# Scale and bias of the activations applied to each tile by ScalarE, in place of scaled PSUM reads and a bias row

## The chip, the cores and the metric

The kernel runs on one core of a Trainium2 chip. The metric is the device time of one execution in microseconds. Before the change it is 912.62 us, the median of three runs (911.99, 912.62, 912.62). The profile shown below is of one further execution, which took 912.49 us; its recorded span is 910.7 us, and the granted TensorE clock was 1.0 over the whole of it.

## The reference

An attention without softmax over 8 batches, 8 heads, 576 tokens and 64 channels feeds a two-layer network over 4608 tokens:

```python
kv  = k.T @ v                                  # per head, over its 576 tokens
out = q @ kv                                   # per head
x   = out / sqrt(mean(out^2) + 1e-6) * g_norm  # then (B, H, S, D) -> (4608, 512)
h   = x @ w_in                                 # (4608, 512) @ (512, 2048)
r   = maximum(h, 0)
g   = s * (r * r) + b                          # s and b: one number each
y   = g @ w_out                                # (4608, 2048) @ (2048, 512)
```

Nearly all the arithmetic is in the two products `x @ w_in` (the first stage) and `g @ w_out` (the second). Since s and b are single numbers, `g @ w_out` equals s times `(r * r) @ w_out` plus b times the column sums of `w_out`: s and b may be applied to the tiles of r*r, or after the second product.

## The kernel before, in words

**Tiling.** The 4608 tokens are 36 chunks of 128, worked on in nine units (0 to 8) of four chunks. In each unit the first stage makes the activations of 512 tokens in four steps of 512 hidden columns; a step gives four tiles, called a11, a12, a21 and a22, of 128 partitions by 512 elements each: two blocks of hidden columns by 256 tokens. (`s` in names such as `s1` counts steps or sums and has nothing to do with the factor s, which stands in `s_col`.) The second stage then multiplies the tiles by w_out.

**Fewer products by the Strassen-Winograd scheme.** A product of matrices cut in 2 x 2 blocks is done as seven products in place of eight, at the price of sums of blocks ahead of and after them. The products are numbered; in a family of seven, products 1, 6, 5 and 3 run into one PSUM bank of tag x, one after the other, each added to what is there, and the bank is read out after each of them; product 2 goes to a bank of tag z; 7 and then 4 go to a bank of tag y. So a bank x that was read by ScalarE or VectorE late makes the next product of its family wait. Unit 0 has a plain first stage (`mm1_plain`, 16 slots, one for each tile, while the weights arrive and are converted from 64 to 32 bits beside it) and one level of the scheme in the second stage. Unit 1 has one level in both (`mm1`, `mm2`). Units 2 to 8 have two levels in the second stage and in part of the first (`mm1_deep`, `at_two_levels`; the weight sums are stored in DRAM once and streamed through a ring of buffers for every unit). There the functions of a family are called `sums_i` (sums of tiles), `do_i` (product and read-out), `go_i` (product alone) and `out_i` (read-out alone), where i is the product of the outer level; `do_1(6)` is inner product 6 of outer product 1.

**Order.** Everything lies under a manual schedule: the program's text fixes the order of instructions of each engine, and an engine takes its own instructions one after the other. Only waits for data and for buffers move things in time. In a deep unit the order is `run` in `mm1_deep` and then `rest` in `mm2`; in units 0 and 1 it is the lists that `mm2` returns and the loop at the end of the kernel. Attention of the next unit is put in between by `at(n)`, by numbered places.

**Activation tiles.** h comes out of PSUM as a sum of what the scheme keeps in tiles. r*r is made in place. On VectorE it is one operation, `relu_sq` (L667, (max(t, 0) times t)). On ScalarE it is a Relu and a Square (L815 and L816 for tiles in SBUF, L861 and L862 for a21 out of PSUM, both in deep units). L849 and L836 are copies of an x bank by ScalarE in a deep unit, L715 is such a copy in unit 1. After r*r come sums of tiles: s1 = a21 + a22 (L250), then differences for the other products (L253). In the deep units a second layer of sums of these (`sums_1`, `sums_25` and so on) is done by VectorE just ahead of the inner products.

**Where s and b enter.** The tiles hold r*r, without s and b. Every read-out of a PSUM bank in the second stage multiplies by s on its way: `scaled` (L1099) is one VectorE operation that computes PSUM times s plus another tile, 128 or 256 elements wide. b enters by a row: `column_sums` adds up the rows of w_out within each partition as the weights of unit 0 arrive (16 operations of VectorE), and `bias_row` (L353 to L361) makes b times the whole column sums of it with one matrix product (into b_ps), a copy to `b_row` (L360) and a difference `b_21` of its halves. `b_row` then is the "other" tile of the first read-outs of every unit, and in deep units `start_5` copies b_21 by ScalarE (L1351) into two quarters of the output tiles, as the value that product 5 starts from. L91 is the one line from which nearly all matmuls are issued.

**Other lines that are spoken of.** L519 scales x by g_norm, four ScalarE operations for 256 tokens. L587 is the Square of the attention's norm. L478 and L568 are parts of the attention. L225 and L230 (ScalarE), L235 and L245 (VectorE) convert the weights in unit 0. The q loads are issued by GpSimd (L1640), as are the stores of the output in units 0 to 7 (L1215).

Of the kernel before, what the change touches and what calls it, by code (L numbers as in the profile page):

```python
# [16 lines left out]
def kernel(  # L17
# [291 lines left out]
    def column_sums(s, lower):  # L309

        w = w_dn if lower else w_up
        for b in range(2):
            f = 2 * s + b
            if f == 0 and not lower:
                nc.vector.tensor_copy(out=b_row, in_=w[:, f])
            else:
                add(b_row, b_row, w[:, f])

# [31 lines left out]
    b_sq = const.tile([P, P], FP32, name="b_sq")  # L350
    nc.vector.memset(b_sq, 1.0)
    b_row = const.tile([P, DM], FP32, name="b_row")
    b_21 = const.tile([P, HN], FP32, name="b_21")  # L353

    def bias_row():

        nc.vector.tensor_scalar(out=b_sq, in0=b_sq, scalar1=b_col, scalar2=None, op0=ALU.mult)
        ps = ps_t.tile([P, DM], FP32, name="b_ps", tag="t")
        matmul(ps, b_sq, b_row, True, True)
        nc.scalar.copy(b_row, ps)  # L360
        sub(b_21, b_row[:, HN:], b_row[:, :HN])  # L361

# [303 lines left out]
    def relu_sq(t):  # L666
        nc.vector.scalar_tensor_tensor(t, t, 0.0, t, ALU.max, ALU.mult)  # L667

# [6 lines left out]
    def g_s1(s):  # L675
        add(ga["s1", s], ga["a21", s], ga["a22", s])

    def mm1_plain(s):


        def block(lower, half, name, tag):
            ps = bank_of("c", tag)
            w = (wb if lower else wa)[s]
            for c in range(KC):
                for b in range(2):
                    matmul(
                        ps[:, b, :], w[:, c, b], xT[0][:, c, half * TB : half * TB + TB],
                        b == 0 and c == 0, c == KC - 1,
                    )
            def out_of():  # L690
                t = g_tile(name, s)
                nc.scalar.activation(t, ps, AF.Relu)
                nc.vector.tensor_mul(t, t, t)

            return out_of

        def c22():
            block(1, 1, "a22", "y")()
            g_tile("s1", s)
            g_s1(s)  # L700

        return [
            lambda: block(0, 0, "a11", "x"),
            lambda: block(1, 0, "a12", "y")(),
            lambda: block(0, 1, "a21", "x")(),
            c22,
        ]

    def mm1(u, s):

        st = {}

        def keep(name, src, tag):
            st[name] = rp.tile([P, 2, TB], FP32, name=name, tag=tag)
            nc.scalar.copy(st[name], src)  # L715

        def x1():
            st["x"] = bank_of("x", "x")
            mm1_product(1, u, s, st["x"], True)
            keep("r1", st["x"], "ra")  # L720

        def z2():
            ps = bank_of("z", "z", 1)
            mm1_product(2, u, s, ps, True)
            t = g_tile("a11", s)
            add(t, ps, st["r1"])
            relu_sq(t)

        def x6():
            mm1_product(6, u, s, st["x"], False)  # L730
            keep("r2", st["x"], "rb")

        def y7():
            st["y"] = bank_of("y", "y")
            mm1_product(7, u, s, st["y"], True)

        def x5():
            mm1_product(5, u, s, st["x"], False)
            keep("r4", st["x"], "ra")
            t = g_tile("a22", s)  # L740
            add(t, st["y"], st["r4"])
            if u > 1 and s == NS - 1:
                nc.scalar.activation(t, t, AF.Relu)
                nc.scalar.square(t, t)
            else:
                relu_sq(t)

        def x3():
            mm1_product(3, u, s, st["x"], False)
            nc.scalar.activation(g_tile("a21", s), st["x"], AF.Relu)  # L750

        def x3_square():
            if u > 1 and s == NS - 1:
                nc.scalar.square(ga["a21", s], ga["a21", s])
            else:
                nc.vector.tensor_mul(ga["a21", s], ga["a21", s], ga["a21", s])

        def x3_s1():
            g_tile("s1", s)
            g_s1(s)  # L760

        def x3_s3():
            sub(ga["a21", s], ga["a11", s], ga["a21", s])

        def y4():
            mm1_product(4, u, s, st["y"], False)
            add(g_tile("a12", s), st["y"], st["r2"])

        def y4_square():
            t = ga["a12", s]  # L770
            if u > 1 and s == NS - 1:
                nc.scalar.activation(t, t, AF.Relu)
                nc.scalar.square(t, t)
            else:
                relu_sq(t)

        return dict(
            x1=x1, z2=z2, x6=x6, y7=y7, x5=x5, x3=x3, x3_square=x3_square, x3_s1=x3_s1,
            x3_s3=x3_s3, y4=y4, y4_square=y4_square,
        )  # L780

# [27 lines left out]
    def mm1_deep(u):  # L809
# [3 lines left out]

        def relu_sq_on_act(t):
            nc.scalar.activation(t, t, AF.Relu)  # L815
            nc.scalar.square(t, t)  # L816
# [34 lines left out]
        def a22(s):  # L851
            t = g_tile("a22", s)
            add(t, st["y", s], ga["a21", s])
            if s == NS - 1:
                relu_sq_on_act(t)
            else:
                relu_sq(t)

        def x3(s):
            mm1_product(3, u, s, st["x", s], False)  # L860
            nc.scalar.activation(ga["a21", s], st["x", s], AF.Relu)  # L861
            nc.scalar.square(ga["a21", s], ga["a21", s])  # L862

        def y4(s):
# [5 lines left out]
            else:  # L870
                relu_sq(t)
# [58 lines left out]

        def done(name, *steps):
# [3 lines left out]
        def run(at, early, sums):  # L935
# [14 lines left out]
            x6(1)  # L950
            small(2, 0, 3, 4)
# [6 lines left out]
            x5(1)  # L958
            a22(1)
# [4 lines left out]
            x1(3)  # L964
            y4(1)
# [5 lines left out]
            x6(2)  # L971
            at(14)
            small(3, 0, 3, 4)
            x6(3)
            done("a21", 0, 1)
            at(15)
            small(2, 1, 1, 2)
            x5(2)
            s1(0)
# [3 lines left out]
            a22(2)  # L983
            y7(3)
# [6 lines left out]
            at(18)  # L991
            y4(2)
            done("a11", 2)
            s1(2)
            x5(3)
            done("a11", 3)
            a22(3)
# [5 lines left out]
            x3_square=lambda: None, y4_square=lambda: None,  # L1003
# [73 lines left out]
    def mm2(u, step=None, side={}):  # L1077
# [20 lines left out]
        def scaled(o, ps, other):  # L1098
            nc.vector.scalar_tensor_tensor(o, ps, s_col, other, ALU.mult, ALU.add)  # L1099

        b1, b2 = b_row[:, :HN], b_row[:, HN:]
# [18 lines left out]
        def at_two_levels(group, other, to):  # L1120
# [48 lines left out]
            def keep(name, j, q):  # L1169
# [4 lines left out]
                scaled(r[name], t["x"], other(j, cols[q]))  # L1174

            def out_of(m, k=slice(0, n)):
                if m == 1:
                    keep("r1", 0, 0)
                elif m == 2:
                    scaled(to(0, cols[0]), t["z"], r["r1"])  # L1180
                elif m == 6:
                    keep("r2", 1, 0)
                elif m == 5:
                    keep("r4", 1, 1)
                    scaled(to(1, cols[1]), t["y"], r["r4"])
                elif m == 3:
                    scaled(to(0, cols[1]), t["x"], other(0, cols[1]))
                elif m == 4:
                    scaled(to(1, cols[0])[:, k], t["y"][:, k], r["r2"][:, k])
# [8 lines left out]
        def part(name, j, ps, other):  # L1198
# [3 lines left out]
            scaled(st[name, j], ps, other)  # L1202
# [19 lines left out]
        def x1(j):  # L1222
            st["x", j] = half(("x", j), "x")
            product(1, j, st["x", j], True)
            if u > 0:
                part("r1", j, st["x", j], b1)

        def early_5(j):
# [3 lines left out]
            nc.scalar.activation(rows("o1", j)[:, HN:], ps, AF.Copy, scale=s_col)  # L1232

        def with_bias():
            bias_row()
            for j in range(2):
                part("r1", j, st["x", j], b1)
            for j in range(2):
                add(st["o1", j][:, HN:], st["o1", j][:, HN:], b2)
            scaled(st["o1", 0][:, :HN], st["z"], st["r1", 0])  # L1240

        def z2(j):
            ps = half("z", "z", 1) if j == 0 else half("z", "y")
            product(2, j, ps, True)
            if u == 0 and j == 0:
                st["z"] = ps
            else:
                scaled(rows("o1", j)[:, :HN], ps, st["r1", j])
# [9 lines left out]
        def x6(j):  # L1258
            product(6, j, st["x", j], False)
            part("r2", j, st["x", j], b1)  # L1260
# [3 lines left out]
        def y7(j):  # L1264
            st["y", j] = half(("y", j), "y")
            product(7, j, st["y", j], True)
            if u == 0:
                scaled(rows("o2", j)[:, HN:], st["y", j], st["r4", j])

        def x5(j):  # L1270
            product(5, j, st["x", j], False)
            part("r4", j, st["x", j], b2)
            scaled(rows("o2", j)[:, HN:], st["y", j], st["r4", j])

        def x3(j):
            product(3, j, st["x", j], False)
            scaled(rows("o1", j)[:, HN:], st["x", j], b2 if u == 1 else st["o1", j][:, HN:])
            store("o1", j, 4 * u + j)

        def y4(j):  # L1280
            product(4, j, st["y", j], False)
            scaled(rows("o2", j)[:, :HN], st["y", j], st["r2", j])
# [19 lines left out]
        if u == 0:  # L1302
# [5 lines left out]
                seq(lambda: z2(0), with_bias),  # L1308
# [39 lines left out]
        def start_5():  # L1348

            for j in range(2):  # L1350
                nc.scalar.copy(slot(j, 3), b_21)  # L1351

        sums_1, go_1, out_1, do_1 = at_two_levels(
            (1,), one(lambda j, q: b1[:, q]), one(lambda j, q: slot(j, 1)[:, q])
# [29 lines left out]
        def rest():  # L1384
            do_1(1)
            step["x3"]()
            step["x3_square"]()
# [143 lines left out]
    def more(n):  # L1531

        s, lower = where(n)
        if n >= 2 * NS:
            column_sums(s, lower)
# [109 lines left out]
    def first_unit():  # L1645
        for n, slot in enumerate(slots0):
            if n > 1:
                out_of = slot()
                if out_of:
                    out_of()  # L1650
            if n in tile_at:
                for step in (hi, lo, shift, plus):
                    step(tile_at[n])
            if n in more_at:
                more(more_at[n])

    def x3(a):
        for name in ("x3", "x3_square", "x3_s1", "x3_s3"):
            a[name]()

    def y4(a):
        for name in ("y4", "y4_square"):
# [160 lines left out]
```

## Time and profile before

Shares are of the recorded span of 910.7 us.

| what | busy us | share | instructions |
|---|---|---|---|
| TensorE, matmuls | 900.6 | 99% | 7524 |
| TensorE, weight loads (overlap matmuls) | 827.4 | 91% | 7524 |
| VectorE | 694.3 | 76% | 1266 |
| ScalarE | 254.0 | 28% | 463 |
| GpSimd (mostly DMA issues) | 223.4 | 25% | 418 |

The chain of work that ended last lies on TensorE for 95% of the span and on VectorE for 3%. DMA moved 180.33 MB, 198 GB/s in the mean. Unit 0 ends and unit 1 begins at about 136.5 us, unit 2 at about 239 us; from there a unit takes about 96 us, with the last one a little shorter.

How to read lines of the trace below: each starts with the start time in us from the span's start, and the duration; then engine, line, operation, output <- inputs with partitions x elements. In brackets stands the time that the engine was idle just before, and whose work ended that. Runs of alike instructions are put together (x8 is eight of them). In a list of waits, the columns are the waiting engine and its output, what released it, and then the idle us, how many such waits there were and the mean of one. For matmuls the start is recorded and the end is modelled, so the end of one can lie behind the start of the next.

### The profile page before, as it was taken

To read this page: it belongs to the slowest core of one execution; us is meant where nothing else is said; L and a number is where in the kernel's file an instruction comes from. 1 tells how busy PE (TensorE), PEld (TensorE's weight loads), DVE (VectorE), ACT (ScalarE), POOL (GpSimd) and SP (SyncE) were. 2 spreads that over 40 slices of the span, in tenths; PEclk is the share of its full clock that TensorE was granted. 3 is DMA by queue.
4 is the path that set the end of the run, shared out by engine and by line. 5 is a ranking of instruction groups with operands and counts; after the bars stand their busy time and mean duration, and the time that the engine had idled before them with its cause. 6 is when DMAs were issued, how large, how long until landed. Compare 5 with 4: busy or idle time off the path is not lost.

```text
span 910.7 us, 19162 instructions
## 1 busy us (share of the span) xinstructions
PE 900.6 (99%) x7524; PEld 827.4 (91%) x7524; DVE 694.3 (76%) x1266; ACT 254.0 (28%) x463; POOL 223.4 (25%) x418
## 2 busy tenths in 40 slices
PE   7999999999999999999999999999999999999998
PEld 7888888888889998999899998999899989999998
DVE  2799678688668986788678858885889778874786
ACT  2874122211135013420334024401450035002400
POOL 2000016113623232810283035503440300020000
PEclk9999999999999999999999999999999999999999
DMA  9687937339943994379626982598438812991286
GB/s 262 223 313 252 263 81 230 101 84 389 339 139 82 285 326 139 77 238 313 199 70 185 302 255 77 128 303 260 128 91 289 283 38 54 280 301 47 56 255 185
DMA packets 120137, 180.33 MB, mean 198 GB/s; under 512 B 29168, under 2 KB 46320, under 8 KB 120048
## 3 DMA queue, kind: packets, MB, share of 16 engines
q1 hardware_dynamic: 101552, 153.00, 53.6%
q0 software_dynamic: 15040, 23.88, 8.7%
q10 hardware_dynamic: 3456, 2.23, 1.0%
q8 instruction: 60, 0.98, 0.4%
q14 instruction: 29, 0.24, 0.1%
HBM read 153.36 MB, written 25.69 MB: 197 GB/s over the span
## 4 chain that ended last, share of the span: by engine, by line
PE 95%; DVE 3%; DMA 1%; ACT 0%; issue 0%; ACTq 0%; DVEq 0%
PE x_ps L91 48%; PE y_ps L91 29%; PE z_ps L91 9%; PE sx_ps L91 4%; PE y_ps L568 2%; DMA kv_sb<-in_v_dram 1%; PE kv_ps L389 1%; PE z_ps L389 1%; DVE sub L253 0%; PE y_ps L389 0%; DVE o L1099 0%; DVE a L253 0%; PE qT_ps L557 0%; DVE xn L478 0%; DVE r L1099 0%
## 5 line engine op out<-in xcount | busy, mean ns | idle before, releaser
L1640 POOL DMA_DIRECT2D q_sb<-in_q_dram x256 | 143.6, 569 | 136.0 <-ACT a L849 63.4
L1215 POOL DMA_DIRECT2D out_dram<-o x110 | 54.8, 505 | 404.1 <-DVE o L1099 281.5
L91 PE MATMUL x_ps<-w_sb,sub 128*128 128x128 f32 x1176 | 149.4, 276 | 0.7 <-DVE r L1099 0.7
L91 PEld LDWEIGHTS x_ps<-w_sb,sub 128*128 128x128 f32 x1176 | 139.7, 192 | 1.8 <-DVE r L1099 1.1
L91 PE MATMUL x_ps<-xs,ws 128*128 128x256 f32 x512 | 121.3, 380 | 0.0
L91 PE MATMUL y_ps<-xs,wb 128*128 128x256 f32 x512 | 120.8, 381 | 0.0
L91 PEld LDWEIGHTS y_ps<-xs,wb 128*128 128x128 f32 x512 | 94.5, 190 | 12.5 <-issue 0.6
L91 PEld LDWEIGHTS x_ps<-xs,ws 128*128 128x128 f32 x512 | 93.9, 190 | 11.4 <-issue 0.4
L91 PE MATMUL x_ps<-xT,wa 128*128 128x256 f32 x384 | 89.0, 381 | 0.1
L836 ACT COPY a<-x_ps 128x512 f32<-128x512 f32 x28 | 16.4, 585 | 255.0 <-PE x_ps L91 255.0
L91 PEld LDWEIGHTS x_ps<-xT,wa 128*128 128x128 f32 x384 | 71.3, 190 | 10.9 <-issue 1.5
L250 DVE TENSOR_TENSOR r<-sx_ps,a 128x256 f32<-128x256 f32 x63 | 26.7, 423 | 65.8 <-PE sx_ps L91 65.7
L91 PE MATMUL x_ps<-w_sb,a 128*128 128x128 f32 (+1 forms) x432 | 64.9, 298 | 0.0
L91 PE MATMUL y_ps<-w_sb,a 128*128 128x128 f32 (+1 forms) x416 | 62.1, 295 | 0.0
L91 PEld LDWEIGHTS x_ps<-w_sb,a 128*128 128x128 f32 x432 | 59.0, 191 | 3.3 <-issue 0.4
L91 PEld LDWEIGHTS y_ps<-w_sb,a 128*128 128x128 f32 x416 | 56.1, 192 | 2.1
L1099 DVE SCALAR_TENSOR_TENSOR r<-x_ps,s_col,o 128x256 f32<-128x256 f32 (+1 forms) x84 | 34.7, 414 | 27.3 <-PE x_ps L91 26.0
L91 PE MATMUL y_ps<-w_sb,sub 128*128 128x128 f32 x392 | 49.6, 275 | 0.0
L253 DVE TENSOR_TENSOR a<-a,a 128x512 f32<-128x512 f32 x72 | 47.4, 684 | 0.4
L91 PE MATMUL z_ps<-w_sb,a 128*128 128x128 f32 (+1 forms) x352 | 46.8, 280 | 0.0
L91 PEld LDWEIGHTS y_ps<-w_sb,sub 128*128 128x128 f32 x392 | 46.6, 192 | 0.1
L91 PEld LDWEIGHTS z_ps<-w_sb,a 128*128 128x128 f32 x352 | 43.9, 192 | 0.8
(196 smaller groups left out, 1488.8 us busy)
## 6 DMA issues: line engine op xcount, KB each, us to landing
w_sb<-w SPq DMA_DIRECT2D x385, 256.0 KB, 4.4
w_raw<-in_moe_w_in_dram SPq DMA_DIRECT2D x8, 1024.0 KB, 7.0
w_raw<-in_moe_w_out_dram SPq DMA_DIRECT2D x8, 1024.0 KB, 4.9
w_sb<-w SPq DMA_DIRECT2D x14, 512.0 KB, 8.5
w<-sub POOLq DMA_DIRECT2D x28, 256.0 KB, 6.6
w_sb<-in_k_dram SPq DMA_DIRECT2D x24, 288.0 KB, 5.0
w_sb<-in_v_dram SPq DMA_DIRECT2D x24, 288.0 KB, 5.2
out_dram<-o POOLq DMA_DIRECT2D x92, 64.0 KB, 3.6
```

The costliest lines, as they stand in the source:

```text
L91: nc.tensor.matmul(o, lhsT=lhsT, rhs=rhs, start=start, stop=stop, skip_group_check=True)
L250: nc.vector.tensor_tensor(out=o, in0=a, in1=b, op=ALU.add)
L253: nc.vector.tensor_tensor(out=o, in0=a, in1=b, op=ALU.subtract)
L389: nc.tensor.matmul(ps[r][(r ^ l) * HB : (r ^ l) * HB + HB, i, :], lhsT=kv[l][0][rows, j, :], rhs=kv[l][1][rows, j, :], start=(j == 0), sto ...
L568: nc.tensor.matmul(ps[l][32 * p : 32 * p + 32, r, lo:hi], lhsT=bd_kv[b % 2][rows, p, at : at + 32], rhs=st["qT"][rows, p, lo:hi], start=Tr ...
L836: nc.scalar.copy(g_tile("a11", s), st["x", s])
L1099: nc.vector.scalar_tensor_tensor(o, ps, s_col, other, ALU.mult, ALU.add)
L1215: queues[s % 2].dma_start(out=view[b, jj, :, cols], in_=st[name, j][s * w : s * w + w, cols])
L1640: load()
```

## The change

s and b are applied to the tiles themselves: after r*r, ScalarE runs `Identity(s_col * t + b_col)` in place on each of the 16 tiles of a unit (`affine`). The second stage then needs no s and no b: a read-out that had another tile to add is a plain addition, and one that only added a bias row is a plain copy. Copies are done by VectorE, except r4 of the two-level families and the read-outs `part` and x3 of the one-level ones, which ScalarE does. The column sums of w_out, `bias_row` with its matmul, and b_21 go away; `start_5` becomes a memset to zero by GpSimd.

Since the affine comes between the square and the sums that use the tile, some operations are moved: in `mm1_plain`, the a12 and a22 tiles' Relu goes from ScalarE to VectorE, the affines of a slot are collected and run at its end (`scale_g`), and s1 of a step comes one slot later; in unit 1, s1 and s3 of a step move from behind x3 to behind y4, and x3's square goes from VectorE to ScalarE; in `run`, the affines of a22 and a12 stand on their own (`scaled("a22", 0)` and so on) one or two places behind the squares on VectorE, and `done("a21", 1)` and `done("a11", 2)` change places with a neighbour.

```diff
-    def column_sums(s, lower):
...
-    def bias_row():
-        nc.vector.tensor_scalar(out=b_sq, in0=b_sq, scalar1=b_col, scalar2=None, op0=ALU.mult)
-        ps = ps_t.tile([P, DM], FP32, name="b_ps", tag="t")
-        matmul(ps, b_sq, b_row, True, True)
-        nc.scalar.copy(b_row, ps)
-        sub(b_21, b_row[:, HN:], b_row[:, :HN])
...
-    def relu_sq(t):
+    def affine(t):
+        nc.scalar.activation(t, t, AF.Identity, scale=s_col, bias=b_col)
+
+    def relu_sq(t, last=True):
         nc.vector.scalar_tensor_tensor(t, t, 0.0, t, ALU.max, ALU.mult)
+        if last:
+            affine(t)
+
+    def relu_sq_on_act(t, src=None):
+        nc.scalar.activation(t, t if src is None else src, AF.Relu)
+        nc.scalar.square(t, t)
+        affine(t)
...
                 t = g_tile(name, s)
-                nc.scalar.activation(t, ps, AF.Relu)
+                if lower:
+                    nc.vector.tensor_scalar(
+                        out=t, in0=ps, scalar1=0.0, scalar2=None, op0=ALU.max
+                    )
+                else:
+                    nc.scalar.activation(t, ps, AF.Relu)
                 nc.vector.tensor_mul(t, t, t)
+                to_scale.append(t)
...
             x6(1)
+            scaled("a22", 0)
             small(2, 0, 3, 4)
...
             x5(1)
+            scaled("a12", 0)
             a22(1)
...
-            done("a21", 0, 1)
+            done("a21", 0)
             at(15)
             small(2, 1, 1, 2)
             x5(2)
+            done("a21", 1)
             s1(0)
...
             at(18)
+            done("a11", 2)
             y4(2)
-            done("a11", 2)
             s1(2)
             x5(3)
             done("a11", 3)
+            scaled("a12", 2)
             a22(3)
             sums()
...
-        def scaled(o, ps, other):
-            nc.vector.scalar_tensor_tensor(o, ps, s_col, other, ALU.mult, ALU.add)
+        def plus_of(o, ps, other, copy=nc.scalar.copy):
+            if other is None:
+                copy(o, ps)
+            else:
+                add(o, ps, other)
...
-                scaled(r[name], t["x"], other(j, cols[q]))
+                plus_of(
+                    r[name], t["x"], other(j, cols[q]),
+                    nc.scalar.copy if name == "r4" else nc.vector.tensor_copy,
+                )
...
             for j in range(2):
-                nc.scalar.copy(slot(j, 3), b_21)
+                nc.gpsimd.memset(slot(j, 3), 0.0)
...
         sums_1, go_1, out_1, do_1 = at_two_levels(
-            (1,), one(lambda j, q: b1[:, q]), one(lambda j, q: slot(j, 1)[:, q])
+            (1,), lambda j, q: None, one(lambda j, q: slot(j, 1)[:, q])
         )
```

More of the change, by code (lines that the diff above doesn't have):

```diff
@@ L307, in w_out_at @@
         return w[:, 2 * s : 2 * s + 2].rearrange("p b n -> p (b n)")
-    def column_sums(s, lower):
[L311 to L317, printed above, removed]
     def sub_w_out(i, a, b, steps=range(NS)):
@@ L349 @@
     nc.gpsimd.dma_start(out=b_col, in_=moe_b.to_broadcast((P, 1)))
[L350 to L353, printed above, removed]
-    def bias_row():
-        nc.vector.tensor_scalar(out=b_sq, in0=b_sq, scalar1=b_col, scalar2=None, op0=ALU.mult)
-        ps = ps_t.tile([P, DM], FP32, name="b_ps", tag="t")
-        matmul(ps, b_sq, b_row, True, True)
-        nc.scalar.copy(b_row, ps)
-        sub(b_21, b_row[:, HN:], b_row[:, :HN])
     def warm(n):
@@ L676, in g_s1, with scale_g @@
         add(ga["s1", s], ga["a21", s], ga["a22", s])
+    to_scale = []
+    def scale_g():
+        while to_scale:
+            affine(to_scale.pop(0))
     def mm1_plain(s):
@@ L699, in c22 @@
             g_tile("s1", s)
-            g_s1(s)
         return [
@@ L741, in x5 @@
             add(t, st["y"], st["r4"])
[L742 to L746, printed above, removed]
+            relu_sq(t)
         def x3():
             mm1_product(3, u, s, st["x"], False)
[L750 to L756, printed above, removed]
+            relu_sq_on_act(g_tile("a21", s), st["x"])
         def x3_s1():
@@ L769, in y4_square @@
         def y4_square():
[L770 to L775, printed above, removed]
+            relu_sq(ga["a12", s])
         return dict(
-            x1=x1, z2=z2, x6=x6, y7=y7, x5=x5, x3=x3, x3_square=x3_square, x3_s1=x3_s1,
-            x3_s3=x3_s3, y4=y4, y4_square=y4_square,
+            x1=x1, z2=z2, x6=x6, y7=y7, x5=x5, x3=x3, x3_s1=x3_s1, x3_s3=x3_s3, y4=y4, y4_square=y4_square,
         )
@@ L812, in mm1_deep @@
         a = {}
-        def relu_sq_on_act(t):
-            nc.scalar.activation(t, t, AF.Relu)
-            nc.scalar.square(t, t)
         def sums_of_x():
@@ L856, in a22 @@
             else:
-                relu_sq(t)
+                relu_sq(t, False)
         def x3(s):
             mm1_product(3, u, s, st["x", s], False)
-            nc.scalar.activation(ga["a21", s], st["x", s], AF.Relu)
-            nc.scalar.square(ga["a21", s], ga["a21", s])
+            relu_sq_on_act(ga["a21", s], st["x", s])
         def y4(s):
@@ L870, in y4 @@
             else:
-                relu_sq(t)
+                relu_sq(t, False)
         def s1(s):
@@ L929, in small, with scaled @@
                     add(to(1, 0), ps, st["q2"])
+        def scaled(name, s):
+            affine(ga[name, s])
         def done(name, *steps):
@@ L964, in run @@
             x1(3)
+            scaled("a22", 1)
             y4(1)
@@ L971, in run @@
             x6(2)
+            scaled("a12", 1)
             at(14)
@@ L983, in run @@
             a22(2)
+            scaled("a22", 2)
             y7(3)
@@ L1002, in mm1_deep @@
             x3=lambda: x3(3), y4=lambda: y4(3), x3_s1=lambda: s1(3), x3_s3=lambda: s3(3),
-            x3_square=lambda: None, y4_square=lambda: None,
+            y4_square=lambda: None,
         )
@@ L1096, in product @@
                 used((u, i, 0), (u, i, 1))
-        def scaled(o, ps, other):
-            nc.vector.scalar_tensor_tensor(o, ps, s_col, other, ALU.mult, ALU.add)
-        b1, b2 = b_row[:, :HN], b_row[:, HN:]
+        def plus_of(o, ps, other, copy=nc.scalar.copy):
[3 more added lines that the diff above has]
+                add(o, ps, other)
         def parts_of_w(i):
@@ L1179, in out_of @@
                 elif m == 2:
-                    scaled(to(0, cols[0]), t["z"], r["r1"])
+                    add(to(0, cols[0]), t["z"], r["r1"])
                 elif m == 6:
@@ L1184, in out_of @@
                     keep("r4", 1, 1)
-                    scaled(to(1, cols[1]), t["y"], r["r4"])
+                    add(to(1, cols[1]), t["y"], r["r4"])
                 elif m == 3:
-                    scaled(to(0, cols[1]), t["x"], other(0, cols[1]))
+                    plus_of(to(0, cols[1]), t["x"], other(0, cols[1]))
                 elif m == 4:
-                    scaled(to(1, cols[0])[:, k], t["y"][:, k], r["r2"][:, k])
+                    add(to(1, cols[0])[:, k], t["y"][:, k], r["r2"][:, k])
             def do(*ms):
@@ L1196, in at_two_levels, with part @@
             return sums, go, out_of, do
-        def part(name, j, ps, other):
+        def part(name, j, ps, other=None):
             if j == 0:
@@ L1201, in part @@
             st[name, j] = st[name][:, j]
-            scaled(st[name, j], ps, other)
+            plus_of(st[name, j], ps, other)
         def rows(name, j):
@@ L1224, in x1 @@
             product(1, j, st["x", j], True)
-            if u > 0:
-                part("r1", j, st["x", j], b1)
+            part("r1", j, st["x", j])
         def early_5(j):
@@ L1231, in early_5 @@
             product(5, j, ps, True)
[L1232 to L1240, printed above, removed]
+            nc.scalar.copy(rows("o1", j)[:, HN:], ps)
         def z2(j):
@@ L1244, in z2 @@
             product(2, j, ps, True)
[L1245 to L1248, printed above, removed]
+            add(rows("o1", j)[:, :HN], ps, st["r1", j])
         def s2(steps=range(NS)):
@@ L1259, in x6 @@
             product(6, j, st["x", j], False)
-            part("r2", j, st["x", j], b1)
+            part("r2", j, st["x", j])
             if u == 0:
@@ L1267, in y7 @@
             if u == 0:
-                scaled(rows("o2", j)[:, HN:], st["y", j], st["r4", j])
+                add(rows("o2", j)[:, HN:], st["y", j], st["r4", j])
         def x5(j):
             product(5, j, st["x", j], False)
-            part("r4", j, st["x", j], b2)
-            scaled(rows("o2", j)[:, HN:], st["y", j], st["r4", j])
+            part("r4", j, st["x", j])
+            add(rows("o2", j)[:, HN:], st["y", j], st["r4", j])
         def x3(j):
             product(3, j, st["x", j], False)
-            scaled(rows("o1", j)[:, HN:], st["x", j], b2 if u == 1 else st["o1", j][:, HN:])
+            plus_of(rows("o1", j)[:, HN:], st["x", j], None if u == 1 else st["o1", j][:, HN:])
             store("o1", j, 4 * u + j)
@@ L1281, in y4 @@
             product(4, j, st["y", j], False)
-            scaled(rows("o2", j)[:, :HN], st["y", j], st["r2", j])
+            add(rows("o2", j)[:, :HN], st["y", j], st["r2", j])
             store("o2", j, 4 * u + 2 + j)
@@ L1307, in mm2 @@
                 lambda: early_5(1),
-                seq(lambda: z2(0), with_bias),
+                lambda: z2(0),
                 seq(lambda: z2(1), t3),
@@ L1386, in rest @@
             step["x3"]()
-            step["x3_square"]()
             step["y4"]()
@@ L1534, in more @@
         if n >= 2 * NS:
-            column_sums(s, lower)
             if not lower:
@@ L1650, in first_unit @@
                     out_of()
+                if n % 4 == 0:
+                    g_s1(n // 4 - 1)
             if n in tile_at:
@@ L1653, in first_unit @@
                     step(tile_at[n])
+            scale_g()
             if n in more_at:
                 more(more_at[n])
+        g_s1(NS - 1)
     def x3(a):
-        for name in ("x3", "x3_square", "x3_s1", "x3_s3"):
-            a[name]()
+        a["x3"]()
     def y4(a):
-        for name in ("y4", "y4_square"):
+        for name in ("y4", "y4_square", "x3_s1", "x3_s3"):
             a[name]()
```

## The prediction

> **What bounds the kernel now.** I read the page first, then the waits of TensorE, then the timeline engine by engine in unit 0, in unit 1, in unit 2 and in unit 4 (one of the seven alike units 2 to 8). The page's first part and TensorE's waits:
>
> ```profile
> PE 900.6 (99%) x7524; PEld 827.4 (91%) x7524; DVE 694.3 (76%) x1266; ACT 254.0 (28%) x463; POOL 223.4 (25%) x418
> ...
> PE x_ps L91 <- DVE r L1099: 0.7, 1, 0.7
> PE y_ps L91 <- DVE wb L245: 0.3, 1, 0.3
> ```
>
> TensorE is busy 99% of the span and its named waits sum to about 6 us, all but 0.7 us of them in the first 32 us. So the time is the matmul work plus every gap that opens between matmuls. ScalarE is idle 72% and VectorE 24%; work on them costs nothing until a matmul waits for it. What decides is how close each hand-over to TensorE is. The closest that I found is in the deep units, here unit 4 (start us, duration, what):
>
> ```profile
> 481.87 0.58 ACT L849 COPY a<-x_ps 128x512 f32<-128x512 f32 x1 [1.90 <-PE x_ps L91]
> 482.35 0.63 ACT L815 ACTIVATE a<-a 128x512 f32<-128x512 f32 x1
> 483.02 0.63 ACT L816 ACTIVATE a<-a 128x512 f32<-128x512 f32 x1
> 483.55 0.61 ACT L815 ACTIVATE a<-a 128x512 f32<-128x512 f32 x1
> ...
> 483.68 0.69 DVE L250 TENSOR_TENSOR sub<-a,a 128x512 f32<-128x512 f32 x1 [0.50 <-ACT a L816]
> 484.41 0.69 DVE L253 TENSOR_TENSOR sub<-sub,a 128x512 f32<-128x512 f32 x1
> 485.13 0.69 DVE L253 TENSOR_TENSOR sub<-a,sub 128x512 f32<-128x512 f32 x1
> 485.74 0.69 DVE L253 TENSOR_TENSOR a<-a,a 128x512 f32<-128x512 f32 x1
> 486.35 0.34 DVE L1099 SCALAR_TENSOR_TENSOR r<-x_ps,s_col,b_row 128x128 f32<-128x128 f32 x1
> ...
> 482.56 1.94 PE L91 MATMUL x_ps<-xT,ws 128*128 128x256 f32 x8
> 486.07 1.05 PE L91 MATMUL z_ps<-w_sb,a 128*128 128x128 f32 x8
> 486.96 1.06 PE L91 MATMUL x_ps<-w_sb,sub 128*128 128x128 f32 x8
> ```
>
> Read it as a chain. ScalarE squares a11 of the last step (483.02); VectorE has waited 0.50 us for that and then runs four sums and r1 without a pause; r1 empties the x bank at 486.69; the matmul of 486.96 (product 6 of `do_1`) adds into that bank, so it may not start earlier. Its room is 486.96 - 486.69 = 0.27 us, of which 0.11 is the hand-over (the copy of 481.87 ends at 482.45, the matmul that waits for it starts at 482.56). Free room: 0.16 us.
>
> **What the Trainium skill says.** "ScalarE: Activation LUTs", section "What ACT_TABLE_LOAD costs": an ACTIVATE takes 186 ns + 0.833 ns per element, about 93 ns more for each per-partition pointer operand, and neighbours overlap by 93 ns. The trace agrees: Relu on 512 elements would be 0.61 (trace 0.61 to 0.63), and four scalings by g_col on 256, one pointer each, would be 1.69:
>
> ```profile
> 458.83 1.70 ACT L519 ACTIVATE xT<-xT,g_col 128x256 f32<-128x256 f32 x4
> ```
>
> The same page, section "Table sets: the hidden batching unit": identity is in every set, so no table load comes in; the trace of before, with one load at its start, has no Identity to show it. "PSUM — Partial Sum Buffer", section "Engine vs sequencer instructions": the queues of ScalarE and VectorE are strict FIFO. The chain above agrees: r1, ready since the matmul of 481.67 ended, stands behind four sums. "VectorE: DVE Perf Modes", section "Mode 2×_2P": the double rate needs SBUF, as PSUM has one read port, so copies out of PSUM gain nothing. The trace agrees (qT_ps copy 0.69 for 512, as an addition).
>
> **The change part by part.**
>
> Added: 144 Identity activations with two pointers (16 tiles a unit, nine units). Estimate by the skill's price: 0.186 + 2 x 0.093 + 0.427 = 0.80 us, 0.71 to the next independent one. From below it is 0.63, the Relu row. I take 0.80, since the one-pointer rows fit. That is 144 x 0.71 = 102 us more on ScalarE, in idle time save where a chain runs through it.
>
> Deep units, the chain above. The affine follows the square by 0.67 (as 482.35 to 483.02): it starts at 483.69, ends at 484.49, the first sum at 484.52 in place of 483.68, a shift of 0.84. r1 moves to 487.19; as a plain copy it takes 0.28 (an addition out of PSUM on 256 takes 0.42 against 0.48 of L1099, so -0.06), ends at 487.47, and the matmul starts at 487.58 in place of 486.96: 0.62 us a unit, 7 x 0.62 = 4.3 us. Ends: 0.45 with an affine of 0.63; 0.68 if r1 gets no shorter.
>
> Unit 2 alone has the attention square behind `at(18)` in this place:
>
> ```profile
> 284.87 1.04 ACT L587 ACTIVATE xn<-q_sb 128x1024 f32<-128x1024 f32 x1
> ...
> 288.06 0.59 ACT L849 COPY a<-x_ps 128x512 f32<-128x512 f32 x1 [0.96 <-PE x_ps L91]
> ```
>
> There two affines (a21 and a11 of step 2, 2 x 0.71) now stand ahead of the copy, with some 0.8 to 0.96 us of idle time to take them: the copy starts near 288.66, and the next product on that bank 0.6 us later. +0.6.
>
> Unit 1. The affine of a11 stands ahead of the r2 copy that x5 waits for:
>
> ```profile
> 141.82 0.69 DVE L667 SCALAR_TENSOR_TENSOR a<-a 128x512 f32<-128x512 f32 x1
> 142.13 0.59 ACT L715 COPY r<-x_ps 128x512 f32<-128x512 f32 x1 [3.10 <-PE x_ps L91]
> 143.65 1.89 PE L91 MATMUL x_ps<-xs,ws 128*128 128x256 f32 x8
> ```
>
> The affine waits for 142.51, the copy follows at 143.25, ends at 143.84, and x5 starts at 143.95 in place of 143.65: +0.3 in step 0. In steps 1 to 3 the same sum leaves 0.2 us or more.
>
> Unit 0. The bias row's matmul goes:
>
> ```profile
> 94.30 3.62 PE L91 MATMUL z_ps<-w_dn,a 128*128 128x256 f32 x16
> 97.75 1.02 PE L91 MATMUL b_ps<-b_row,b_sq 128*128 128x512 f32 x2
> 98.61 3.62 PE L91 MATMUL y_ps<-w_dn,a 128*128 128x256 f32 x16
> ```
>
> 98.61 - 97.75 = -0.86 us, sure, as it lies between two products. The column sums (16 operations of 0.42 to 0.7 on VectorE) and b_21 save nothing: TensorE ran through beside them. The affines fit: a slot lasts 3.45 us, ScalarE had about 2.1 for a weight tile and 0.5 for a Relu; half the Relus go to VectorE, which loses more in column sums; so about 3.1 of 3.45. Weight tile 3, the one in most danger, is ready about 40.2, used at 42.28.
>
> Second stage, other units. L1099 becomes an addition (-0.06 us each) or a copy. That matters only where TensorE waits for one: in unit 2,
>
> ```profile
> 314.52 1.16 PE L91 MATMUL x_ps<-w_sb,sub 128*128 128x128 f32 x8 [0.67 <-DVE r L1099]
> ```
>
> seven L1099 stand in the unbroken VectorE run before it (from 306.75): -0.4; a smaller gap at 324.84 closes: -0.2; and each deep unit has one step of 0.185 between matmuls in place of 0.112 (525.44 in unit 4), where three or four shorter ones come before: 7 x 0.07 = -0.5. Edits I cost at nothing: the copies r4 and x3 on ScalarE (r4 starts about 491.2 behind the affine of a12, ends at 491.5, its bank is next written at 492.0), the memset on GpSimd in place of the b_21 copies (it stands behind the q loads, which end at 487.5 in unit 4; the first reader is at 492.4), the moved s1 and s3 (their VectorE run catches up at 477.97 and each bank is read out 0.2 us or more before its next matmul).
>
> Sum: 4.3 + 0.6 + 0.3 - 0.86 - 0.6 - 0.5 = +3.2. 912.6 + 3.2 = **915.9 us**.
>
> **Rivals.**
> - Hidden after all, faster: for it speaks ScalarE's 72% idle time; against it the 0.16 us of room. Only the savings remain: -0.86 - 0.6 - 0.5, 910.7 us.
> - Short affines (0.63) and a little more room than the modelled ends show: 7 x 0.45 + 0.4 + 0.1 - 1.96 = +1.7, 914.3 us, within 0.2%.
> - Further waits: the places costed at nothing have 0.2 to 0.5 us of room on my sums. If one of them misses by 0.5 in each deep unit: +3.5 more, 919.4 us. For it: three new waits of VectorE on ScalarE (s1 of steps 0 and 1, the addition after r4). Against it: VectorE idles 0.2 to 0.7 us several times just behind them.
>
> **How the numbers follow.** Forecast 0.62, faster 0.08, short affines 0.15, further waits 0.15. The range leaves out the faster case and the far part of the last: 912.3 to 919.0. Slower by over 0.2% (above 914.4): forecast, further waits and a small part of the third, 0.78; within 0.2%, 0.14; faster, 0.08.
>
> **What would show it.** In each deep unit the matmul of product 6 in `do_1` waits about 0.6 us for r of VectorE; an Identity takes 0.80; unit 2's x3 of step 3 waits 0.6 us for the copy; b_ps is gone, with 0.86 us; 314.52's wait is shorter. The forecast fails if Identity takes 0.6, if r1 is not what the matmul waits for, or if TensorE shows gaps in other places: then look at the r4 copy and at s1.

## The result and the profile after

The changed kernel takes 915.0 us (median of nine runs, 914.63 to 915.26) against 912.62 us before (median of nine, 911.99 to 912.96): a ratio of 1.0027, with a 95% interval from 1.0017 to 1.0037. It is slower, by 2.4 us; the forecast was 3.2 us and 915.9. The profiled span is 913.3 us, 2.6 more than before.

The page of the changed kernel, its first part, and TensorE's waits (what waited, for what; total us, count, longest; the last column is the longest wait, in the lists shown further up too, and not the mean):

```profile
PE 899.8 (99%) x7522; PEld 826.3 (90%) x7522; DVE 662.4 (73%) x1223; ACT 364.3 (40%) x614; POOL 228.3 (25%) x432
...
PE x_ps L91 <- DVE r L1087: 2.9, 7, 0.4
...
PE x_ps L91 <- ACT a L827: 0.4, 1, 0.4
```

VectorE lost 32 us of work and ScalarE gained 110, and the span grew all the same. Two kinds of wait are new and say why: seven waits for the copy r1 (L1087), one in each of units 2 to 8, and one for a copy by ScalarE (L827), in unit 2. (The wait of 0.7 us for L1099 is now one of 0.2 for the addition L250.) Unit 4 of the changed kernel, on ScalarE, VectorE and TensorE:

```profile
483.13 0.63 ACT L653 ACTIVATE a<-a 128x512 f32<-128x512 f32 x1
483.80 1.52 ACT L644 ACTIVATE a<-a,b_col,s_col 128x512 f32<-128x512 f32 x2
...
484.64 0.69 DVE L250 TENSOR_TENSOR sub<-a,a 128x512 f32<-128x512 f32 x1 [1.35 <-ACT a L644]
485.37 0.69 DVE L253 TENSOR_TENSOR sub<-sub,a 128x512 f32<-128x512 f32 x1
486.09 0.69 DVE L253 TENSOR_TENSOR sub<-a,sub 128x512 f32<-128x512 f32 x1
486.70 0.68 DVE L253 TENSOR_TENSOR a<-a,a 128x512 f32<-128x512 f32 x1
487.30 0.28 DVE L1087 COPY r<-x_ps 128x128 f32<-128x128 f32 x1
...
487.64 1.16 PE L91 MATMUL x_ps<-w_sb,sub 128*128 128x128 f32 x8 [0.41 <-DVE r L1087]
```

This is the chain that the prediction drew. VectorE idles 1.35 us where it idled 0.50, then four sums, then r1, then the matmul. Read the last line twice: the bracket shows 0.41 us, but the group takes 1.16 us where it took 1.06. The listed 0.41 us is counted from the modelled end of the matmul before; by the recorded starts, the interval between the two is 0.68 us where it was 0.11, so the matmul starts 0.57 later. One more interval, behind that matmul, is 0.21 in place of 0.11. So all that follows comes 0.67 later.

The matmuls of both kernels stand in the same order but for b_ps (and some pairs of neighbours in the attention that change places), so each can be set beside its twin, and the difference of start times sums up all that happened. The steps in that difference are:

| place (time in the trace before) | what | step, us | forecast |
|---|---|---|---|
| unit 0, 98.61 | the matmul b_ps is gone | -0.86 | -0.86 |
| unit 1, 140.12 | a gap ahead of x6 closed | -0.18 | none |
| unit 1, 143.65 | r2's copy behind an affine | +0.33 | +0.3 |
| unit 2, 288.75 | x5's copy behind two affines | +0.63 | +0.6 |
| units 2 to 8, 486.96 in unit 4 | r1 behind the sums, behind the affine | +4.72 (7 x 0.67 to 0.69) | +4.3 |
| unit 2, 314.52, 322.72, 324.84 | three waits for read-outs shorter | -0.84 | -0.6 (without 322.72) |
| units 2 to 8, 525.44 in unit 4 | a gap ahead of inner product 5 closed | -1.22 (7 x 0.17 to 0.18) | -0.5 |
| start of unit 0, and elsewhere | loads, and drifts of at most 0.06, within what differs from run to run | +0.08 | none |
| sum | | +2.66 | +3.2 |

### The profile page after: what moved, and what is told of

It is laid out like the page before. It is cut to its first block, busy times and chain, and to the rows that moved or that the text cites. A ratio compares the mean times of both kernels' runs of the same rounds, so it can differ in the third digit from the quotient of the medians.

```text
span 913.3 us, 19278 instructions
## 1 busy us (share of the span) xinstructions
PE 899.8 (99%) x7522; PEld 826.3 (90%) x7522; DVE 662.4 (73%) x1223; ACT 364.3 (40%) x614; POOL 228.3 (25%) x432
## 5 line engine op out<-in xcount | busy, mean ns | idle before, releaser
L644 ACT ACTIVATE a<-a,b_col,s_col 128x512 f32<-128x512 f32 x144 | 116.2, 812 | 29.4 <-DVE a L647 23.2
L250 DVE TENSOR_TENSOR r<-sx_ps,a 128x256 f32<-128x256 f32 x63 | 26.6, 422 | 62.1 <-PE sx_ps L91 61.9
L250 DVE TENSOR_TENSOR r<-x_ps,o 128x256 f32<-128x256 f32 (+1 forms) x84 | 29.7, 354 | 32.7 <-PE x_ps L91 30.6
L653 ACT ACTIVATE a<-a 128x512 f32<-128x512 f32 x74 | 46.7, 630 | 2.4
```

The lines of the kernel that those rows point to most:

```text
L250: nc.vector.tensor_tensor(out=o, in0=a, in1=b, op=ALU.add)
L644: nc.scalar.activation(t, t, AF.Identity, scale=s_col, bias=b_col)
```

## The experiments

Times are medians of 4 to 21 runs. The kernel before was run beside each group, at 912.61, 912.62 and 912.46 us. Where a step is given in a trace, it is the difference of twin matmuls' start times against the changed kernel.

### r1 ahead of the sums

```diff
-            "sums": lambda: (start_5(), sums_1((5, 6, 3))),
+            "sums": start_5,
...
         def rest():
             do_1(1)
+            sums_1((5, 6, 3))
```

(so s3 of step 2 and r1 come ahead of the three sums that wait for the affine)

> The changed kernel with one order altered in the seven deep units: the difference s3 of step 2 and the copy r1 of do_1 are queued on VectorE ahead of the three sums that wait for the affine of a11, not behind them. Theory (the seven waits for r1 cost 0.67 us each with the restart behind them): 915.0 - 4.7 = 910.3 us, and TensorE shows no wait for the r1 copy any more. Rival A (the affine delays the sums as well, and product 6, which uses the second of them, then waits in place of r1): a wait for sub of VectorE of 0.3 us or more in each deep unit, 912.5 to 915. Rival B (the waits were hidden by work that only moved): 915.0.

Measured: 911.77 us, ratio to before 0.9991 (0.9984 to 0.9997). The mechanism stands: none of the seven waits for L1087 is left, and each unit gains 0.67 to 0.69 us there. The number fell short: 3.2 us gained, not 4.7. The rest was given back in a place that neither theory named, 4.5 us later in each deep unit. Unit 4, the affine of a12 of step 3 and the copy r4 on ScalarE, the addition behind r4 on VectorE, and inner product 3 of `do_1` on TensorE, which adds into the bank that r4 reads:

```profile
489.80 0.81 ACT L644 ACTIVATE a<-a,b_col,s_col 128x512 f32<-128x512 f32 x1
490.52 0.24 ACT L1087 COPY r<-x_ps 128x128 f32<-128x128 f32 x1
...
490.80 0.29 DVE L250 TENSOR_TENSOR o<-y_ps,r 128x128 f32<-128x128 f32 x1 [1.49 <-ACT r L1087]
...
490.82 1.16 PE L91 MATMUL x_ps<-w_sb,sub 128*128 128x128 f32 x8
```

ScalarE works without a pause from 481.24 to 490.76 here: x5's copy, three operations for each of four tiles, one more affine, then r4. That queue starts when x5's product is done and gets no shorter when TensorE comes earlier. With r1 early, TensorE reaches product 3 just when r4 ends, and loses 0.13 us a unit, 0.9 in all; in unit 2, where the attention's row sum follows on VectorE, another 0.5. The 0.03 us that the first matmul waits are not listed as a wait; the 1.16 in place of 1.06 shows them.

### The same order in the kernel before

> The same altered order in the kernel before, as a control. Theory (there r1 was in time by 0.16 us, so nothing waits for it): no change, 912.6 within 0.5. Rival (the early r1 gains by itself, whatever the affine does): as much as it gains in the changed kernel, 908 to 909.

Measured: 912.71 us, ratio 1.0 (0.9991 to 1.0008). So the early r1 is worth nothing by itself; in the changed kernel it repays what the affine took.

### A second dose

```diff
             done("a11", 3)
+            nc.scalar.activation(ga["a11", 3], ga["a11", 3], AF.Identity, scale=one_col, bias=zero_col)
```

> The changed kernel with a second Identity (times one, plus zero) behind the affine of a11 of step 3 in each of the seven deep units. Theory (ScalarE's square and affine of that tile, then VectorE's sums, then r1, then the matmul are one chain): each unit gets longer by the pitch of an affine, 0.72 us, 7 x 0.72 = 5.0: 920.0 us, and the wait for r1 is 1.1 us. Rival (VectorE is late for a cause of its own, a copy or an addition out of PSUM that takes longer): the second Identity lies in idle time, 915.0.

Measured: 922.22 us, ratio 1.0106 (1.0093 to 1.012), more than expected. The trace splits it: 0.83 to 0.85 us in each deep unit (5.90 in all; the second Identity starts 0.84 us behind the one that it depends on, not 0.72), and 1.24 us in unit 0, where a load of q came later and TensorE waited 1.0 us for it. The run was done again with the affine itself applied twice:

```diff
             done("a11", 3)
+            affine(ga["a11", 3])
```

> The dose test again, without new constants: the affine of a11 of step 3 applied a second time in each deep unit, with the same pointers (so s and b are in that tile twice, which changes the output). It was 922.2 us with the constants one and zero, of which the trace put 5.86 in the seven waits (0.84 each, as the second Identity depends on the first and starts 0.84 behind it, not 0.72) and 1.24 in a later start of unit 0. Theory: without the two new constants the later start is gone, 915.0 + 5.9 = 920.9. Rival (the 1.24 belong to the longer chain in some way): 922.2.

Measured: 920.92 us, ratio 1.0091 (1.0075 to 1.0106). Its lines in unit 4, three Identities in a row on ScalarE, the first sum on VectorE and the matmul:

```profile
485.29 2.36 ACT L644 ACTIVATE a<-a,b_col,s_col 128x512 f32<-128x512 f32 x3
...
486.98 0.69 DVE L250 TENSOR_TENSOR sub<-a,a 128x512 f32<-128x512 f32 x1 [2.19 <-ACT a L644]
...
489.99 1.16 PE L91 MATMUL x_ps<-w_sb,sub 128*128 128x128 f32 x8 [1.25 <-DVE r L1088]
```

VectorE's idle time grows from 1.35 to 2.19 us and TensorE's wait from 0.41 to 1.25, both by 0.84: what ScalarE adds to this tile passes through to TensorE whole. The rival, a delay of VectorE's own making, is out. The 1.3 us between the two runs fits the later start of unit 0; why two more constants went with it was not tried.

### No affine at all

```diff
     def affine(t):
-        nc.scalar.activation(t, t, AF.Identity, scale=s_col, bias=b_col)
+        pass
```

> The changed kernel with no affine at all; this leaves out s and b, and what stays is what the change removes and shortens. Theory, from the shifts between the two traces (the bias matmul 0.86, a gap in unit 1 0.16, three waits in unit 2 0.78, one closed gap in each deep unit 7 x 0.18): 912.6 - 3.1 = 909.5 us. Rival A (the affines also delay work that no wait shows): below 909. Rival B (the read-outs are not what closed the gaps, the later start of the units was): 911.8, the bias matmul alone.

Measured: 909.35 us, ratio 0.9963 (0.995 to 0.9975). This splits the change in two: what it removes and shortens saves 912.62 - 909.35 = 3.3 us; the affines cost 915.0 - 909.35 = 5.65 us. The trace against the changed kernel has steps in nine places, and behind the start of unit 0 no other of more than 0.03 us: 0.33 in unit 1, 0.63 in unit 2, and the seven of 0.67 to 0.69.

### Scaled read-outs put back

```diff
+        def add_ps(o, ps, other):
+            nc.vector.scalar_tensor_tensor(o, ps, s_col, other, ALU.mult, ALU.add)
...
-                add(o, ps, other)
+                add_ps(o, ps, other)
...
-                    add(to(0, cols[0]), t["z"], r["r1"])
+                    add_ps(to(0, cols[0]), t["z"], r["r1"])
```

(and so for the other additions out of PSUM in `mm2`)

> The changed kernel with the 84 and more additions out of PSUM turned back into the scaled form of before (PSUM times s plus the other tile; s is so applied twice, which changes the output); the affines, the copies and the missing bias row stay. Theory (the shorter read-outs closed the gaps in unit 2, 0.78, and one in each deep unit, 7 x 0.18): these come back, 915.0 + 2.0 = 917.0 us. Rival (those gaps closed because TensorE came later, behind its new waits, not because read-outs are shorter): 915.0.

Measured: 917.61 us, ratio 1.0054 (1.004 to 1.0068): 2.6 us more than the changed kernel, where 2.0 was expected. The steps lie where the theory put them: 0.19 at x6 in unit 1, 0.84 at the three places in unit 2, 0.16 to 0.18 once in each deep unit; 0.18 more came in two places that were not named. In unit 4 the product that takes 1.16 at 525.44 before takes 1.06 in the changed kernel; with the scaled read-outs it takes 1.16 again. TensorE before:

```profile
525.44 1.16 PE L91 MATMUL x_ps<-w_sb,sub 128*128 128x128 f32 x8
```

with the scaled read-outs:

```profile
527.86 1.16 PE L91 MATMUL x_ps<-w_sb,sub 128*128 128x128 f32 x8
```

and in the changed kernel:

```profile
526.16 1.06 PE L91 MATMUL x_ps<-w_sb,sub 128*128 128x128 f32 x8
```

So the shorter read-outs are what closed these gaps. The rows of the two kernels (mean ns of one): before, the scaled form,

```profile
L1099 DVE SCALAR_TENSOR_TENSOR o<-y_ps,s_col,r 128x128 f32<-128x128 f32 x56 | 19.5, 347 | 1.4 <-PE y_ps L91 0.7
```

and after, the addition that took its place, 0.06 us shorter (the 10.4 us in its row are VectorE's idle time for r4, which is now a copy by ScalarE):

```profile
L250 DVE TENSOR_TENSOR o<-y_ps,r 128x128 f32<-128x128 f32 x56 | 16.1, 287 | 11.8 <-ACT r L1087 10.4 <-PE y_ps L91 0.9
```

### The Identity without pointers

```diff
-        nc.scalar.activation(t, t, AF.Identity, scale=s_col, bias=b_col)
+        nc.scalar.activation(t, t, AF.Identity)
```

> The changed kernel with each affine an Identity without the two pointers; this leaves out s and b. Theory by the Trainium skill's price (93 ns a pointer): an Identity of 0.63 us in place of 0.81, so the chain in each deep unit gets shorter by 0.18, 7 x 0.18 = 1.3, unit 2's two affines ahead of its copy give 0.2 to 0.3 back and unit 1 0.1 to 0.2: 913.4 us. Rival (pointers cost nothing, the 0.81 is Identity's own): 915.0 with an Identity of 0.81.

Measured: 913.05 us, ratio 1.0005 (0.9997 to 1.0013). The Identity takes 0.63 us (median of 144) where the one with two pointers takes 0.81: 0.09 a pointer. This agrees with the Trainium skill ("ScalarE: Activation LUTs", section "What ACT_TABLE_LOAD costs"), which has 93 ns. Each deep unit gains 0.18 to 0.19, unit 2's copy 0.38, twice 0.18 and a little, since two affines stand ahead of it.

### r4 on VectorE, alone

```diff
-                    nc.scalar.copy if name == "r4" else nc.vector.tensor_copy,
+                    nc.vector.tensor_copy,
```

> The changed kernel with the copy r4 of do_1 on VectorE in place of ScalarE, alone. Theory (with TensorE late by its wait for r1 the r4 copy is in time, it becomes a wait only once r1 is early): 915.0 within 0.5. Rival (VectorE's 1.49 us of idle time for r4 already costs in the changed kernel): 913.5 to 914.2.

Measured: 914.94 us, ratio 1.0026 (1.0016 to 1.0035). Nothing, as the theory has it: VectorE's 1.49 us of idle time for r4 costs nothing as long as TensorE comes late.

### Four edits together

The r1 order and r4 on VectorE as above, and:

```diff
             add(t, ps, st["r1"])
-            relu_sq(t)
+            relu_sq(t, False)
...
             keep("r2", st["x"], "rb")
+            affine(ga["a11", s])
...
             scaled("a22", 2)
+            at(17)
...
-                18: [B["square"]],
+                17: [B["square"]],
```

> The changed kernel with four edits: r1 and s3 early as in the first experiment, the copy r4 of do_1 on VectorE, unit 1's affine of a11 behind the copy r2, and unit 2's attention square ahead of the Relu of a21 of step 2. Theory (all waits that the affines made are named, and the first experiment lost 0.13 in each deep unit and 0.55 in unit 2 to the r4 copy behind ScalarE's affines): all of the affines' cost is undone, so the time of the kernel with no affine at all, 909.4 us, 0.35% under the kernel before. Rival (r4 on VectorE delays the sums of product 2 and 5, a new wait there): 911 to 912, no better than the first experiment.

Measured: 909.47 us, ratio 0.9966 (0.9953 to 0.9978). That is the 909.35 of the kernel with no affine, within the spread of the runs: but for one step of 0.33 us, in unit 2, all that the affines cost is gone. The edits act in different places, so the trace tells their shares apart: 0.33 in unit 1, 0.62 at unit 2's copy, and 0.67 to 0.69 in each deep unit, where the 0.13 that the early r1 alone gave back does not come again. Unit 4 in the trace, the same stretch as above:

```profile
488.11 0.81 ACT L644 ACTIVATE a<-a,b_col,s_col 128x512 f32<-128x512 f32 x1
...
487.53 0.28 DVE L1089 COPY r<-x_ps 128x128 f32<-128x128 f32 x1
487.85 0.29 DVE L250 TENSOR_TENSOR o<-y_ps,r 128x128 f32<-128x128 f32 x1
488.95 0.69 DVE L250 TENSOR_TENSOR sub<-a,a 128x512 f32<-128x512 f32 x1 [0.81 <-ACT a L644]
```

r4 (487.53) no longer stands behind the affine of a12 (488.11). The sums of product 2 still wait for that affine, and that costs nothing.

### The row sum of unit 2 earlier

```diff
+            at("s1")
             step["x3_s1"]()
...
-                0: [B["row_sum"]], 1: [A["scale"]], 2: [B["norm"]], 3: [B["turn_x"], *q[1]],
+                "s1": [B["row_sum"]], 1: [A["scale"]], 2: [B["norm"]], 3: [B["turn_x"], *q[1]],
```

> The four edits, and in unit 2 the attention's row sum on VectorE ahead of s1 of step 3 in place of behind the sums of products 2 and 5. Theory (the 0.33 us that remain in unit 2 at the first product on xT-independent sums, near 300.9 in the trace of the four edits, are VectorE's 1.21 us of row sum ahead of them): that gap closes, 909.5 - 0.3 = 909.2 us by the trace, too little for the timed runs to show. Rival (the row sum only moves its delay to s1 or to r4): 909.5 or more, with a new gap between 294 and 297.

Measured: 909.22 us, ratio 0.9963 (0.995 to 0.9975). In the trace the step of unit 2 closes, by 0.36 us. The median is the lowest of all, 5.8 us under the changed kernel and 3.2 under the kernel before that ran beside it; its 0.25 us below the four edits lie within the spread of the runs, so that only the trace shows this last step.

## Why the prediction was right, point by point

- **What bounds, and the chain in the deep units: right, slightly too small.** The term "7 x 0.62" measured 0.67 to 0.69 each, 4.72 in all. The shift of the first matmul was a little overestimated: it is 0.57 to 0.58, as the matmul starts 0.06 us behind the end of r1, not the 0.11 that the prediction took from a copy by ScalarE (so the free room was 0.21, not 0.16). The 0.10 us behind a wait, the longer second interval, was left out. The early r1, its control and the second dose show the mechanism.
- **Price of the affine: right.** Forecast 0.80, measured 0.81. No table load came with it: each trace has one. The rival of short affines gave 914.3; the run without pointers shows what such affines would have done, 913.05.
- **Unit 2's copy (+0.6), unit 1's r2 (+0.3), b_ps (-0.86): right**, each within 0.03 us in the trace.
- **Savings of shorter read-outs: right in place, too small.** The term "7 x 0.07" for the deep units measured 0.17 to 0.18 each, 1.22 in place of 0.5; unit 2's waits gave 0.84 in place of 0.6, and unit 1's 0.18 was not seen. The cause is the same 0.10 us in reverse: a gap of 0.185 that closes to 0.112 takes the longer second interval with it. These terms are why 915.0 came out below 915.9. The chain was put 0.4 us too low and the savings some 1.1 us too low; that the two misses have opposite signs, and in part cancel in the total, is luck.
- **Edits costed at nothing: right in the changed kernel.** No matmul waits for r4, s1, the memset or the weight tiles; r4 on VectorE alone changed nothing. The "thin room" of r4, 0.5 us by the prediction's reckoning, was real: 0.70 us lie between the end of r4 and product 3 in the changed kernel (491.51 and 492.21), and once TensorE came 0.67 us earlier it was used up. (Product 3 of `do_1` is in the deep units read out by a copy of ScalarE as well, seven in all, which the description of the change leaves out; no matmul waits for it.)
- **The rivals.** "Hidden after all" put the savings alone at 910.7; without affines they came to 909.35. It did not happen in the changed order, but four edits, three of order and one of engine, reach it. "Further waits" did not happen.

## What to carry to other kernels

Idle time of an engine says nothing about whether work added to it is free: ScalarE was idle 72% of the span, and 0.81 us in one place, with 0.21 us of room behind it, cost 0.67 us in each of seven units. Look for what stands behind the added operation in the queue of every engine on its way; where a ready operation (here r1) stands behind ones that now wait, move it ahead of them, and then read the trace again, since the next hand-over in line (here r4) may have only as much room as the first wait gave it. A change of this kind should be split before it is judged: its removed half was worth 3.3 us, its added half cost 5.65, and the second could be hidden almost whole.

## What the hardware showed that was not expected

- A wait of TensorE delays what follows by 0.10 us more than it delays the first matmul: in streams of 128-column fp32 matmuls, the interval behind the first matmul after a wait was 0.21 us in place of 0.11 (in all seven units the first matmul came 0.57 to 0.58 later and the second 0.67 to 0.68). The same holds for gaps of 0.07 us that no list of waits shows; a group of eight at 1.16 in place of 1.06 is their mark.
- An Identity that depends on the one before it starts 0.84 us behind it (three in a row, the second on the tile of the first, took 2.36 us); two on different tiles start 0.71 apart (1.52 for two). The overlap of 93 ns between neighbours that the Trainium skill gives ("ScalarE: Activation LUTs", section "What ACT_TABLE_LOAD costs") was seen for independent ones alone.
